# A block-sparse attention layer with two MLPs on one core: float64 weight words converted by whole blocks in place, their flush test from ScalarE's square, the first pass's low weight parts on VectorE

## The chip, the cores and the metric

The kernel runs on one core of a Trainium2 chip. The metric is the device time of one execution in microseconds (us); three runs gave 776.76 (median), 774.83 and 783.42.

## The reference

Three layers follow each other. First comes attention over 2 batches, 8 heads, 768 tokens and a head size of 64, in which a query sees only the keys that fall to the same of 16 centroids. Then comes a Fourier mixing with an MLP of width 2048, and last an MLP of width 1024 with a convolution of three taps and a gate:

```python
x = attn_out.transpose(0, 2, 1, 3).reshape(B, S, H * D)        # (2, 768, 512)
u = x + np.real(np.fft.fft(np.fft.fft(x, axis=1), axis=2))
un = (u - mean(u)) / np.sqrt(var(u) + 1e-06)
x = u + np.maximum(un @ w_ch1, 0.0) @ w_ch2                    # 512 -> 2048 -> 512
h = np.maximum(x @ w_in, 0.0)                                  # 512 -> 1024
conv_out = conv of h along the tokens, three taps per channel
out = (h * sigmoid(conv_out)) @ w_out                          # (2, 768, 512)
```

The weights of both MLPs and the taps come to the kernel as float64 (the draw makes them so), and are passed as pairs of 32-bit words.

## The kernel before, in words

**Stages.** Attention of all 16 heads is issued in an order written out by hand: 96 steps of 128 rows, and dictionaries (pre, mid, aft, post, fill) that hang other work on a step. Batch 0's mixing and normalisation are hung on the last third of these steps. Behind attention the order is made by the framework's planner: the program order is the priority, and the planner places each instruction in its engine's queue by its own estimate of when operands and buffers come free. Each engine then works its queue strictly in order.

**The wide MLP** goes in two passes, one per batch (g = 0, 1), over 16 weight blocks f. A block holds 128 columns of w_ch1 and 128 rows of w_ch2, as one tile of 128x1024. Precision comes from three matmuls in place of one (`pass3`, lines 75 to 78): high x high, high x low, low x high, where the high part is a value rounded to float32r and the low part the rest. `split_w` (line 763) makes the two weight parts: ScalarE casts the block (line 765), GpSimd subtracts (line 767). `mlp1_up` does 24 matmuls of 384 columns, ScalarE's ReLU gives the high part (line 781), VectorE subtracts for the low part (line 782). `down` does 18 matmuls of 512 columns into six banks. So a block of a pass has 42 matmuls. In pass 0 batch 1's mixing and normalisation are spread between the blocks (`later`): 30 matmuls for three `y` (lines 141 and before), 18 for two `z`, 7 and 39 for `a384` and three `ab`, and 24 transposes (line 261). Its folds, low parts and additions lie on VectorE and GpSimd (lines 104 to 222), its high parts on ScalarE (lines 113, 143, 145, 173). In pass 1 the second layer's transposes (`gate_in`) lie between the blocks. The last layer (`mlp2_up`, 8 blocks per batch) splits its blocks the same way.

**Conversion.** `from64` (line 273) makes float32 from the two words w0 (low) and w1 (high) of each float64. Its five VectorE steps are: the exponent and mantissa bits of w1, shifted, into a scratch tile `cvt` (line 277); the sign joined to it (278); the top three bits of w0 joined, into the target (279); w1 without its sign, into the scratch tile (281); a test of that against 0x38100000, multiplied with the target, so that what float32 could hold only as a denormal becomes zero (282). Lines 277 and 281 read one tensor, the others two. `load_w` (line 290) loads and converts a block in two halves of 512 columns, with three buffers `raw64` of 4 KB per partition and one scratch tile. Blocks a2 to a15 (the trace's `rawa`, `wa`) are converted in pass 0, blocks b0 to b7 of the last layer (`rawb`, `wb`) in pass 1. `NA` gives 2, 7 and 7 places for converted blocks; a9 to a15 use memory that batch 1's mixing gives up, and b0 and b1 take the places of a0 and a1 behind their last split. Blocks a0 and a1 are converted half by half during attention (`ahead_start`, line 660 on), a step of `from64` at each of five steps of the order, and go out to DRAM and back; a0's parts are made by `first_split`.

```python
AHEAD_STEPS = [12 * q + n for q in range(4) for n in (9, 10, 15, 17, 18)]
```

Of the kernel before, what the change touches and what calls it, by code (L numbers as in the profile page):

```python
# [12 lines left out]
I32 = mybir.dt.int32  # L13
U32 = mybir.dt.uint32
I64 = mybir.dt.int64
AF = mybir.ActivationFunctionType
ALU = mybir.AluOpType
# [8 lines left out]
AHEAD_STEPS = [12 * q + n for q in range(4) for n in (9, 10, 15, 17, 18)]  # L26
# [4 lines left out]
NT = S // 128  # L31
NH = B * H
BIG = float(2.0 ** 100)
P_SHIFT = 11

C_CS, C_SS, C_CD, C_SD, C_END = 0, 1158, 2310, 2826, 3342
# [4 lines left out]
def tile_net(ctx, tc, qk, v, cen, w12, w34, conv, dft, odd, out):  # L41
    nc = tc.nc
    V, A, G, T = nc.vector, nc.scalar, nc.gpsimd, nc.tensor

    def f32(ap):
        return ap.bitcast(F32)
# [13 lines left out]
    cbias = cp.tile([128, 1], F32, name="cbias")  # L60
    V.memset(cbias, float(P_SHIFT * np.log(2.0)))

    def pool(ctx_, name, bufs=1, side="left"):
        return ctx_.enter_context(tc.tile_pool(name=name, bufs=bufs, side=side, reuse_waits="tile"))
# [205 lines left out]
    NA = (2, 7, 7)  # L270
    wst, cvs, w32 = [], [], {}

    def from64(dst, raw, t):

        w0, w1 = (raw.rearrange("p (n t) -> p n t", t=2)[:, :, i] for i in range(2))
        return (
            lambda: V.tensor_scalar(t, w1, 3, 0x3FFFFFFF, ALU.logical_shift_left, ALU.bitwise_and),
            lambda: V.scalar_tensor_tensor(t, w1, -0x40000000, t, ALU.bitwise_and, ALU.bitwise_or),  # L278
            lambda: V.scalar_tensor_tensor(dst.bitcast(U32), w0.bitcast(U32), 29, t.bitcast(U32),  # L279
                                           ALU.logical_shift_right, ALU.bitwise_or),  # L280
            lambda: V.tensor_scalar(t, w1, 0x7FFFFFFF, None, ALU.bitwise_and),  # L281
            lambda: V.scalar_tensor_tensor(dst, t, float(0x38100000), dst, ALU.is_ge, ALU.mult),
        )

    def place_w(k, f):
        part = 0 if f < NA[0] else 1 if f < NA[0] + NA[1] else 2
        w32[k, f] = wst[part].tile([128, 1024], F32, tag="w32", bufs=NA[part], name=f"w{k}{f}")
        return w32[k, f]

    def load_w(k, f):  # L290
        w = place_w(k, f)
        for i in range(2):
            raw = cvs[0].tile([128, 1024], I32, tag="raw64", bufs=3, name=f"raw{k}{f}{i}")
            sl = slice(512 * i, 512 * i + 512)
            nc.sync.dma_start(out=raw.bitcast(I64), in_=(w12 if k == "a" else w34)[f][:, sl])
            for op in from64(w[:, sl], raw, cvs[0].tile([128, 512], I32, tag="cvt", bufs=1, name="cvt")):
                op()

    def up_half(o, w, x, i):
        tk = slice(384 * i, 384 * i + 384)  # L300
        for c in range(4):
            sl = slice(128 * c, 128 * c + 128)
            pass3(o, w[0][:, sl], w[1][:, sl], x[:, 0, c, tk], x[:, 1, c, tk], c == 0, c == 3)

    ws, hs, acc, xs, gps = {}, {}, {}, {}, []


    with ExitStack() as actx:
# [7 lines left out]
        def slot(name):  # L316
            turn[0] = (turn[0] + 1) % 3
            return ps.tile([128, 2, 512], F32, tag=f"s{turn[0]}", bufs=1, name=name)
# [37 lines left out]
        t = slot("warm_up")  # L356
# [22 lines left out]
        for i in range(2):  # L379
            t = ap.tile([128, NT, 2, 130], F16, name=f"V16_{i}")  # L380
# [30 lines left out]
        def prep_turn(m, t):  # L411
# [5 lines left out]
            A.copy(o[:, 0], po[0])  # L417
            A.activation(o[:, 1], po[1], AF.Copy, bias=-BIG, scale=BIG)
            d = ohD[m] = dr.tile([96, 2, 2, 128], F32, tag="ohd", name=f"ohd{m}")
            nc.sync.dma_start(out=d, in_=o)  # L420

        def first_mask():
# [6 lines left out]
            A.copy(Xs[0][64:80, 0], po[0])  # L429
            V.tensor_scalar(Xs[0][64:80, 1], po[1], BIG, -BIG, ALU.mult, ALU.add)  # L430

# [151 lines left out]
        def attn_out(hh, i):  # L583
            b, h = hh // 8, hh % 8
            r = avs[hh][:, 0:390].rearrange("p (t c) -> p t c", t=6)
            if i == 0:
                d = ds[hh] = ap.tile([128, 6], F32, tag="d", bufs=2, name=f"d{hh}")
                V.tensor_scalar(d, r[:, :, 64], float(2.0 ** P_SHIFT * 1e-9), None, ALU.add)
            elif i == 1:
# [9 lines left out]
        def at(where, step, *f):  # L599
            where.setdefault(step, []).append(f)  # L600

        for m in range(1, NH // 2):
            k = 12 * m - 24
# [45 lines left out]
        for i, t in enumerate((0, 3, 1, 4, 2, 5)):  # L649
            n = 72 + 3 * i  # L650
# [8 lines left out]
        def ahead_start(q):  # L659
            if q == 0:  # L660
                t = up_[0].tile([128, 8, S], F32R, tag="un", bufs=1, name="ahead")
                ahead["t"] = f32(t).rearrange("p a s -> p (a s)")
            t, f, i = ahead["t"], q // 2, q % 2
            raw = t[:, 1024 * i:1024 * i + 1024].bitcast(I32)
            nc.sync.dma_start(out=raw.bitcast(I64), in_=w12[f][:, 512 * i:512 * i + 512])
            dst = ahead[q] = t[:, 2560 + 512 * q:3072 + 512 * q]
            for n, op in zip(AHEAD_STEPS[5 * q:], from64(dst, raw, t[:, 2048:2560].bitcast(I32))):
                at(aft, n, op)

        def ahead_store(q):  # L670
# [7 lines left out]
        for q in range(AHEAD):  # L678
            at(pre, AHEAD_STEPS[5 * q] - 2, ahead_start, q)
            at(pre, AHEAD_STEPS[5 * q + 4] + 1, ahead_store, q)  # L680
# [45 lines left out]
        for n in range(-LEAD, 6 * NH + 10):  # L726
# [13 lines left out]
            if n in DFT_LOADS:  # L740
                i = DFT_LOADS.index(n)
# [10 lines left out]
    wp = pool(ctx, "wp", side="right")  # L752
    wst.append(pool(ctx, "wstA", side="right"))
    hctx = ctx.enter_context(ExitStack())
    hp = pool(hctx, "hp", side="right")
# [4 lines left out]
    def up_bank(name):  # L760
        return bank("up", 2, name)

    def split_w(p, bufs, k, f, name):
        wh = p.tile([128, 1024], F32R, tag="wh", bufs=bufs, name=f"wh{name}")
        A.copy(wh, w32[k, f])  # L765
        wl = p.tile([128, 1024], F32R, tag="wl", bufs=bufs, name=f"wl{name}")
        G.tensor_sub(wl, w32[k, f], f32(wh))  # L767
        return wh[:, 0:512], wl[:, 0:512], wh[:, 512:1024], wl[:, 512:1024]

    def mlp1_up(g, f):  # L770
        if (g, f) == (0, 0):
            h = hs[0, g, f] = [dp.tile([128, 780], F32R, tag=t, bufs=1, name=f"first{t}")[:, 0:S] for t in ("e0", "e1")]
            w = ws[0, g, f]
        else:
            h = hs[0, g, f] = [hp.tile([128, S], F32R, tag=t, bufs=3, name=f"{t}{g}_{f}") for t in ("hH", "hL")]
            w = ws[0, g, f] = split_w(hp, 3, "a", f, f"a{g}_{f}")
        for i in range(2):
            o = up_bank(f"up{g}_{f}_{i}")[:, 0:384]
            up_half(o, w, uns[g], i)
            tk = slice(384 * i, 384 * i + 384)  # L780
            A.activation(h[0][:, tk], o, AF.Relu)  # L781
            V.scalar_tensor_tensor(h[1][:, tk], o, 0.0, f32(h[0][:, tk]), ALU.max, ALU.subtract)  # L782
# [21 lines left out]
    def down(s, g, f, side, when=(2,)):  # L804
        w, h = ws.pop((s, g, f)), hs.pop((s, g, f))
        last = (15, 7)[s]
        if f == 0:
            acc[s, g] = [bank(f"acc{t}", 1, f"acc{s}{g}{t}") for t in range(NT)]
        for t in range(NT):
            sl = slice(128 * t, 128 * t + 128)  # L810
            pass3(acc[s, g][t], h[0][:, sl], h[1][:, sl], w[2], w[3], f == 0, f == last)
            if t in when and side:
                next(side, None)
            if f == last:
                if s == 0:
                    V.tensor_add(U[:, 6 * g + t], U[:, 6 * g + t], acc[s, g][t])
                else:
                    y = gps[0].tile([128, 512], F32, tag="y", bufs=3, name=f"y{g}{t}")
                    if t % 2:
                        V.tensor_copy(y, acc[s, g][t])  # L820
                    else:
                        A.copy(y, acc[s, g][t])
                    nc.sync.dma_start(out=out[g, 128 * t:128 * t + 128], in_=y)
# [41 lines left out]
    cw = wp.tile([128, 24], F32, tag="cw", bufs=1, name="cw")  # L865
    craw = wp.tile([128, 48], I32, tag="craw", bufs=1, name="craw")
    nc.sync.dma_start(out=craw.bitcast(I64), in_=conv)
    side = later()
    mlp1_up(0, 0)
    load_w("a", 2)  # L870
    for g in range(B):
        for f in range(16):
            if (g, f) < (B - 1, 15):
                mlp1_up(*((g, f + 1) if f < 15 else (g + 1, 0)))
            if (g, f) == (B - 1, 15):
                next(side, None)
            down(0, g, f, side, (1, 4) if g == 0 else (2,))
            if g == 0 and f + 3 < 16:
                load_w("a", f + 3)
            if g == 1 and 1 <= f < 9:  # L880
                load_w("b", f - 1)
            if (g, f) == (0, 15):
                side = gate_in(0)
            if (g, f) == (1, 9):
                for op in from64(cw, craw, wp.tile([128, 24], I32, tag="ccvt", bufs=1, name="ccvt")):
                    op()
    hctx.close()
    gps.append(pool(ctx, "gp", side="right"))
# [79 lines left out]
```

## Time and profile before

| | |
|---|---|
| median of three runs | 776.76 us |
| the profiled execution, its own time | 775.36 us |
| its span, first to last instruction | 773.6 us |
| TensorE matmul / VectorE / ScalarE / GpSimd busy | 703.1 / 581.5 / 314.8 / 358.3 us |
| mean granted TensorE clock | 0.974 |

The profile names engines PE (TensorE), PEld (its weight loads), DVE (VectorE), ACT (ScalarE), POOL (GpSimd) and SP (the DMA queue). Attention ends at about 305 us of the span, pass 0 at about 484, pass 1 at about 621. L279 is line 279 of the kernel. Busy times say little by themselves over the whole span, since the stages have different limits; the sections below look at single stages.

### The profile page before, as it was taken

How to read it: one execution, taken by the hardware profiler on the slowest of the kernel's cores; microseconds unless marked ns; L12 is line 12 of the kernel's file. 1: busy time of each engine (PE TensorE's matmuls, PEld its weight loads, DVE VectorE, ACT ScalarE, POOL GpSimd, SP SyncE). 2: the span in 40 equal slices, each digit the busy share in tenths (PEclk: the TensorE clock that was granted, in tenths of full speed). 3: DMA queues.
4: the chain of work that ended last, by engine and by line, in shares of the span. 5: the costliest groups of instructions: out<-in, count | busy, mean ns of one | idle time of the engine just before them, and what ended most of it. 6: DMA issues, size and time to landing. Idle time of an engine off the chain costs nothing.

```text
span 773.6 us, 12743 instructions
## 1 busy us (share of the span) xinstructions
PE 703.1 (91%) x5082; PEld 623.9 (81%) x5082; DVE 581.5 (75%) x864; ACT 314.8 (41%) x458; POOL 358.3 (46%) x231
## 2 busy tenths in 40 slices
PE   6899898997898897987998999999999989999996
PEld 5688797887797786876997789888999978888984
DVE  8668789898868999989669996999211167777763
ACT  2476667585457683222222212222222323333231
POOL 6276677577357765432353223222232155444441
PEclk9999999999899998988999999999999999999999
DMA  7768675552533330223203332231000000001002
GB/s 203 174 186 240 149 183 145 130 154 69 135 69 89 78 136 6 108 81 111 81 28 109 108 112 89 101 123 68 1 1 1 1 0 1 1 1 74 8 1 82
DMA packets 23107, 66.49 MB, mean 86 GB/s; under 512 B 3220, under 2 KB 6280, under 8 KB 22792
## 3 DMA queue, kind: packets, MB, share of 16 engines
q1 hardware_dynamic: 22616, 61.93, 27.9%
q0 software_dynamic: 432, 3.75, 1.4%
q8 instruction: 40, 0.66, 0.4%
q14 instruction: 19, 0.16, 0.1%
HBM read 40.94 MB, written 5.77 MB: 60 GB/s over the span
## 4 chain that ended last, share of the span: by engine, by line
PE 43%; DVE 40%; issue 5%; DMA 4%; POOL 4%; ACT 3%; SPq 1%; POOLq 0%; DVEq 0%; ACTq 0%
PE acc L76 4%; PE acc L78 4%; PE acc L77 4%; DVE cvt L278 4%; PE av L580 4%; DVE m L523 3%; DVE wa L279 3%; PE up L76 3%; PE s L518 3%; PE up L77 3%; PE up L78 3%; PE t L552 3%; DVE cvt L281 2%; PE t L554 2%; PE s L520 2%
## 5 line engine op out<-in xcount | busy, mean ns | idle before, releaser
L568 POOL TENSOR_TENSOR p<-p,p 128x768 f16<-128x768 f32 x76 | 135.4, 1787 | 80.2 <-ACT p L563 50.0
L767 POOL TENSOR_TENSOR wla<-wa,wha 128x1024 fp32r<-128x1024 f32 x31 | 79.4, 2562 | 172.7 <-ACT wha L765 172.7
L556 ACT ACTIVATE p<-t,cbias 128x768 f32<-128x768 f32 x96 | 86.3, 899 | 62.8 <-PE t L554 54.6
L523 DVE TENSOR_REDUCE m<-s 128x1 f32<-128x768 f32 x96 | 90.1, 944 | 14.8 <-PE s L520 14.2
L76 PE MATMUL up<-un,wha 128*128 128x384 f32 x248 | 86.1, 347 | 6.3 <-DVE Zy L152 5.2
L78 PE MATMUL up<-un,wla 128*128 128x384 f32 x248 | 84.6, 341 | 3.7 <-POOL wla L767 3.7
L77 PE MATMUL up<-un,wha 128*128 128x384 f32 x248 | 84.3, 340 | 0.0
L782 DVE SCALAR_TENSOR_TENSOR hL<-up,hH 128x384 fp32r<-128x384 f32 x62 | 34.2, 552 | 65.1 <-ACT hH L781 65.1
L580 PEld LDWEIGHTS <-p 128*128 128x128 f16 x1728 | 61.2, 100 | 22.3 <-issue 15.5
L580 PE MATMUL av<-V,p 128*128 128x65 f16 x1728 | 73.2, 197 | 6.1 <-POOL p L568 4.4
L563 ACT CAST p<-p 128x768 f16<-128x768 f32 x91 | 75.6, 831 | 1.6
L76 PE MATMUL acc<-wha,hH 128*128 128x512 f32 x186 | 74.1, 398 | 0.0
L77 PE MATMUL acc<-wla,hH 128*128 128x512 f32 x186 | 72.8, 391 | 0.0
L78 PE MATMUL acc<-wha,hL 128*128 128x512 f32 x186 | 72.7, 391 | 0.0
L552 PE MATMUL t<-X 128*128 128x384 f32 x192 | 55.6, 371 | 18.5 <-DVE m L523 17.6
L781 ACT ACTIVATE hH<-up 128x384 fp32r<-128x384 f32 x62 | 30.1, 490 | 96.3 <-PE up L78 96.3
L518 PE MATMUL s<-X 128*128 128x384 f32 x192 | 57.7, 382 | 8.3 <-DVE m L523 2.7
L765 ACT CAST wha<-wa 128x1024 fp32r<-128x1024 f32 x31 | 32.6, 1051 | 78.5 <-PE acc L78 42.4
L799 POOL TENSOR_TENSOR cv<-cv,h 128x768 f32<-128x768 f32 x16 | 25.4, 1591 | 78.1 <-ACT cv L798 78.1
L801 DVE CAST gH<-cv 128x768 fp32r<-128x768 f32 x16 | 35.3, 2208 | 31.3 <-POOL cv L799 28.7
L76 PEld LDWEIGHTS up<-un,wha 128*128 128x128 f32 x248 | 47.1, 190 | 11.3 <-DVE Zy L152 5.5
L552 PEld LDWEIGHTS t<-X 128*128 128x128 f32 x192 | 32.4, 195 | 25.4 <-DVE m L523 18.6
(310 smaller groups left out, 1684.2 us busy)
## 6 DMA issues: line engine op xcount, KB each, us to landing
rawa<-w SPq DMA_DIRECT2D x28, 512.0 KB
rawb<-w SPq DMA_DIRECT2D x16, 512.0 KB
raw<-qk SPq DMA_DIRECT2D x7, 768.0 KB
X<-G SPq DMA_DIRECT2D x14, 384.0 KB
Y<-G SPq DMA_DIRECT2D x14, 384.0 KB
DC<-dft POOLq DMA_DIRECT2D x2, 1671.0 KB, 9.1
vraw<-v SPq DMA_DIRECT2D x8, 384.0 KB
out<-y SPq DMA_DIRECT2D x12, 256.0 KB
```

Of the source, the lines that this page charges most:

```text
L76: T.matmul(o, sH, mH, start=start, stop=False)
L77: T.matmul(o, sH, mL, start=False, stop=False)
L78: T.matmul(o, sL, mH, start=False, stop=stop)
L518: T.matmul(t[:, c, 0:384], X[:, 0, sl], X[:, 1, 384 * c:384 * c + 384], start=True, stop=False)
L523: V.tensor_reduce(m6s[h][:, i:i + 1], t[:, :, 0:384], AX.XY, ALU.max, negate=True)
L552: T.matmul(t[:, c, 0:384], X[:, 1, sl], X[:, 0, 384 * c:384 * c + 384], start=True, stop=False)
L556: A.activation(p.rearrange("p (c n) -> p c n", c=2), t[:, :, 0:384], AF.Exp, bias=cbias, scale=0.125)
L563: A.copy(p16[:, 0], p32s[n])
L568: eng.tensor_sub(p16[:, 1], p, p16[:, 0])
L580: T.matmul(o, p16[:, k, 128 * j:128 * j + 128], v16[:, i, h % 2, 65 * part:65 * part + 65], start=(i + j + k + part == 0), stop=(i == 5), ...
L767: G.tensor_sub(wl, w32[k, f], f32(wh))
L801: V.tensor_copy(g[0], t)
```

## The change

Four things change. `from64` has no scratch tile: its first two steps write the target itself. Its fourth step, the mask on VectorE, goes; instead ScalarE squares w1, read as a float32, in place, ahead of the third step, and the last step tests the square against `LEAST` (the square of the float that has the bits 0x38100000, made smaller by 2^-16 of itself). `load_w` loads and converts a whole block of 1024 columns at a time, with two buffers of 8 KB per partition. `split_w` gets an engine for the subtraction: VectorE in pass 0, GpSimd in pass 1 and in the last layer. In attention the five steps of a half fall on the same five places: first, second, square, third, last.

```diff
+LEAST = float((1.125 * 2.0 ** -15) ** 2 * (1 - 2.0 ** -16))
...
-    def from64(dst, raw, t):
+    def from64(dst, raw):
...
+        d = dst.bitcast(I32)
         return (
-            lambda: V.tensor_scalar(t, w1, 3, 0x3FFFFFFF, ALU.logical_shift_left, ALU.bitwise_and),
-            lambda: V.scalar_tensor_tensor(t, w1, -0x40000000, t, ALU.bitwise_and, ALU.bitwise_or),
-            lambda: V.scalar_tensor_tensor(dst.bitcast(U32), w0.bitcast(U32), 29, t.bitcast(U32),
+            lambda: V.tensor_scalar(d, w1, 3, 0x3FFFFFFF, ALU.logical_shift_left, ALU.bitwise_and),
+            lambda: V.scalar_tensor_tensor(d, w1, -0x40000000, d, ALU.bitwise_and, ALU.bitwise_or),
+            lambda: A.activation(f32(w1), f32(w1), AF.Square),
+            lambda: V.scalar_tensor_tensor(dst.bitcast(U32), w0.bitcast(U32), 29, dst.bitcast(U32),
                                            ALU.logical_shift_right, ALU.bitwise_or),
-            lambda: V.tensor_scalar(t, w1, 0x7FFFFFFF, None, ALU.bitwise_and),
-            lambda: V.scalar_tensor_tensor(dst, t, float(0x38100000), dst, ALU.is_ge, ALU.mult),
+            lambda: V.scalar_tensor_tensor(dst, f32(w1), LEAST, dst, ALU.is_ge, ALU.mult),
         )
...
     def load_w(k, f):
         w = place_w(k, f)
-        for i in range(2):
-            raw = cvs[0].tile([128, 1024], I32, tag="raw64", bufs=3, name=f"raw{k}{f}{i}")
-            sl = slice(512 * i, 512 * i + 512)
-            nc.sync.dma_start(out=raw.bitcast(I64), in_=(w12 if k == "a" else w34)[f][:, sl])
-            for op in from64(w[:, sl], raw, cvs[0].tile([128, 512], I32, tag="cvt", bufs=1, name="cvt")):
-                op()
+        raw = cvs[0].tile([128, 2048], I32, tag="raw64", bufs=2, name=f"raw{k}{f}")
+        nc.sync.dma_start(out=raw.bitcast(I64), in_=(w12 if k == "a" else w34)[f])
+        for op in from64(w, raw):
+            op()
...
-    def split_w(p, bufs, k, f, name):
+    def split_w(p, bufs, k, f, name, eng=G):
...
-        G.tensor_sub(wl, w32[k, f], f32(wh))
+        eng.tensor_sub(wl, w32[k, f], f32(wh))
...
-            w = ws[0, g, f] = split_w(hp, 3, "a", f, f"a{g}_{f}")
+            w = ws[0, g, f] = split_w(hp, 3, "a", f, f"a{g}_{f}", (V, G)[g])
```

The other two calls of `from64` (in `ahead_start` and for the taps) lose their scratch tile in the same way.

## Rows read from the trace of the kernel before

**Rows 1.** Busy time by stretch: length, PE, PEld, DVE, ACT, POOL (instructions), PE clock, DMA

```profile
305.00:485.00 180.00, 164.20 (x835) 147.31 (x836) 154.46 (x246) 42.26 (x70) 64.19 (x36) 0.95 0.25 91
325.00:365.00 40.00, 29.92 (x130) 26.16 (x129) 36.89 (x52) 7.15 (x12) 14.45 (x7) 0.83 0.25 90
365.00:405.00 40.00, 40.00 (x223) 37.22 (x223) 26.17 (x53) 10.25 (x19) 17.36 (x13) 1.00 0.16 59
405.00:465.00 60.00, 54.36 (x275) 46.88 (x275) 58.56 (x90) 15.10 (x24) 17.19 (x8) 1.00 0.31 110
485.00:545.00 60.00, 57.06 (x291) 49.71 (x290) 57.48 (x88) 16.77 (x27) 17.21 (x7) 1.00 0.25 88
550.00:575.00 25.00, 25.00 (x128) 22.82 (x127) 3.34 (x6) 6.10 (x9) 7.19 (x3) 1.00 0.00 1
```

**Rows 2.** Chain of waits, 349 to 362 us: start, length, engine, output, line

```profile
352.06 2.73 DVE wa L279
...
356.45 0.56 DVE Zy L152
...
357.06 0.69 PE up L76
```

**Rows 3.** Waits, 305 to 485 us: who waited for whom, us in total, times, longest

```profile
ACT hH L781 <- PE up L78: 51.3, 23, 8.7
ACT wha L765 <- DVE wa L282: 33.9, 10, 7.5
PE up L76 <- DVE Zy L152: 5.2, 1, 5.2
PEld up L78 <- POOL wla L767: 5.0, 4, 2.1
DVE wb L279 <- POOL wla L767: 5.0, 1, 5.0
PEld y L76 <- ACT EH L113: 3.7, 1, 3.7
PEld y L78 <- POOL EL L117: 2.0, 1, 2.0
```

**Rows 4.** Busy time of conversion steps (tile `cvt`): first weights, then second

```profile
285.00:463.80 178.80, 106.46 (x140) 0.94 0.23 83
463.80:545.00 81.20, 58.30 (x81) 1.00 0.26 91
```

**Rows 5.** Tiles `rawa`, `wa`: ns minimum/median/maximum, first and last start, shape

```profile
L277 DVE TENSOR_SCALAR cvt<-rawa x28: 399/427/430, 288.8 to 460.4; 128x512 int32<-128x512 int32 x28
L279 DVE SCALAR_TENSOR_TENSOR wa<-rawa,cvt x28: 666/693/2837, 306.7 to 461.9; 128x512 uint32<-128x512 uint32 x28
L765 ACT CAST wha<-wa x31: 1036/1050/1058, 301.2 to 600.3; 128x1024 fp32r<-128x1024 f32 x31
L767 POOL TENSOR_TENSOR wla<-wa,wha x31: 2354/2466/3086, 304.2 to 601.5; 128x1024 fp32r<-128x1024 f32 x31
L692 DVE CAST firstYsH<-wa x1: 412/412/412, 300.8 to 300.8; 128x512 fp32r<-128x512 f32 x1
```

**Rows 6.** Instructions in order of time, 406 to 412 us: start, length, engine, line

```profile
407.69 2.35 POOL L767 TENSOR_TENSOR wla<-wa,wha 128x1024 fp32r<-128x1024 f32 x1 [4.91 <-ACT wha L765]
407.75 2.84 DVE L279 SCALAR_TENSOR_TENSOR wa<-rawa,cvt 128x512 uint32<-128x512 uint32 x1
```

**Rows 7.** Tile `G`: VectorE steps of 768 elements, columns as in rows 5

```profile
L443 DVE CAST G<-raw x7: 541/1610/2009, 5.5 to 236.8; 128x768 fp32r<-128x768 f32 x7
L448 DVE TENSOR_TENSOR G<-raw,G x7: 945/957/1055, 6.1 to 240.9; 128x768 fp32r<-128x768 f32 x7
```

**Rows 8.** Tile `rawa`, 310 to 315 us: length, DVE busy, PE clock, DMA share, GB/s

```profile
310.00:315.00 5.00, 3.40 (x6) 1.00 0.47 172
```

**Rows 9.** VectorE's groups by shape: count, busy us, mean ns

```profile
L281 DVE TENSOR_SCALAR ahead<-ahead 128x512 int32<-128x512 int32 x4 | 4.1, 1026 | 0.0
```

**Rows 10.** ScalarE's groups by shape

```profile
L798 ACT ACT_TABLE_LOAD x1 | 1.3, 1283 | 0.0
```

More of the change, by code (lines that the diff above doesn't have):

```diff
@@ L666, in ahead_start @@
             dst = ahead[q] = t[:, 2560 + 512 * q:3072 + 512 * q]
-            for n, op in zip(AHEAD_STEPS[5 * q:], from64(dst, raw, t[:, 2048:2560].bitcast(I32))):
+            for n, op in zip(AHEAD_STEPS[5 * q:], from64(dst, raw)):
                 at(aft, n, op)
@@ L884, in tile_net @@
             if (g, f) == (1, 9):
-                for op in from64(cw, craw, wp.tile([128, 24], I32, tag="ccvt", bufs=1, name="ccvt")):
+                for op in from64(cw, craw):
                     op()
```

## The prediction

> **What bounds the kernel now.** I read the time by stages first. In the first pass of the wide MLP (305 to 485 us) VectorE works 154.5 of 180 us and TensorE stands idle 15.8; TensorE's granted clock is 0.95 of the higher of its two levels (1.2 and 2.4 GHz) there, and 0.83 from 325 to 365, where 10.1 of the 15.8 idle us lie. From 405 to 465 VectorE works 58.6 of 60 us, TensorE 54.4. From 550 to 575, where VectorE has almost nothing to do, TensorE has no gap: 128 matmuls in 25 us, 0.195 us each, 8.2 us for the 42 of one weight block [rows 1].
>
> Next I ask what TensorE waits for. In the piece of the chain of waits from 349 to 362 us, conversion steps stand ahead of VectorE's small step on line 152, and TensorE resumes right behind it [rows 2]. The list of waits for the pass says the same: 5.2 us for line 152; ScalarE waits 33.9 us in 10 places for the last conversion step (line 282) before it can split the next block [rows 3]. So the pass is bound by VectorE's queue, not by TensorE's arithmetic. That arithmetic is 16 blocks x 8.2 = 131 us, 94 matmuls of batch 1's mixing and 24 transposes at no more than 0.195 = 23 [rows 1], in all 154. The pass has 26 us of slack: 15.8 of idle, 5 to 8 of low clock, the rest in gaps too short for the view.
>
> Then what fills VectorE: five conversion steps for each half block, 106.5 us for the first weights and 58.3 for the second [rows 4]. One half costs 0.43 + 3 x 0.69 + 0.43 = 2.93 us at the medians (the steps that read one tensor, lines 277 and 281, have one median, those that read two, lines 278, 279 and 282, the other), so 28 halves should take 82 us. The other 24.5 are steps that took up to 2.84 us [rows 5]. One of these shows why: GpSimd starts a weight subtraction at 407.69 and ends at 410.04; VectorE's line 279 starts at 407.75 and takes 2.84 instead of 0.69 [rows 6].
>
> **The change part by part.** *Whole blocks, one step fewer.* A step of 1024 has no row here. The one-source step goes from 0.41 (512, line 692) to 0.54 (768, line 443), 0.50 ns an element, so 0.43 + 512 x 0.50 = 0.69 us. The two-source steps go from 0.69 (512) to 0.96 (768), 1.04 ns an element, so 1.23 us [rows 5, 7]. A block then costs VectorE 0.69 + 3 x 1.23 = 4.4 us, where two halves cost 5.8. For 14 blocks this is 61; doubling the half steps gives 70, and no price per instruction would give 52. I take 61, since both slopes come from the nearest sizes. Against 106.5 this saves 45 us, of which 5 come back where GpSimd's mixing steps still stretch VectorE's.
>
> *Low weight parts on VectorE in the first pass.* Fifteen subtractions of 1024 at 1.23 add 18.5 us to VectorE and take 15 x 2.47 = 37 us off GpSimd [rows 5], and with them most of the stretching counted above. VectorE's busy time goes from 154.5 to 154.5 - 106.5 + 61 + 5 + 18.5 = 133 us (bounds 124 and 148) against TensorE's 154: it would no longer be the bound, but it would still be 87% full. The new subtraction waits for ScalarE's cast; behind it in VectorE's queue stand conversions and line 782, for which TensorE's next matmuls wait.
>
> *The square on ScalarE.* One square per block: 1.05 us by the cast of 1024 [rows 5], 14 x 1.05 = 15 us on an engine that is busy 42 of 180 us in the pass [rows 1]. It overwrites the words that VectorE's first two steps read, so it waits for them, and behind it stand ScalarE's ReLUs and casts; VectorE's last step waits for it, with line 782 behind. A wait of this kind has no row. Bounds: nothing, where the square runs beside the third step (1.05 under 1.23), and 8.7 us, the longest wait of a ReLU for TensorE [rows 3] with a square behind it. I take nothing, because ReLUs wait 2.2 us in the mean (51.3 over 23) and other VectorE steps can stand between.
>
> The Trainium skill's "ScalarE: Activation LUTs" (Rules for kernel authors) advises VectorE over ScalarE for simple arithmetic. Here the step leaves VectorE at 2 x 0.43 and costs ScalarE 1.05 [rows 5]: dearer, but on the idler engine. By that rule keeping it would cost VectorE 14 x 0.69 = 10 us in the pass and leave 143 of 154.
>
> *In place.* The first two steps now write the block's own place. For the first second-layer block that place was free only after GpSimd's subtraction; the third step waited 5.0 us for it, with VectorE idle [rows 3]. Now the first step waits there, with line 782 behind it; this idle time covers the two steps that can no longer go ahead, and I count nothing (without it, 0.69 + 1.23 = 1.9 us, once).
>
> *Transfers.* 22 issues of 1 MB replace 44 of half that, two buffers of 8 KB replace three of 4. The same bytes move. From 310 to 315 us the transfers ran at 172 GB/s with half of the engines' time unused [rows 8]; at that rate a block takes 6.1 us and two buffers give one each (4.4 + 6.1) / 2 = 5.3 us, under the 8.2 in which TensorE uses one. Cost nothing; at worst some 3 us ahead of the first block, covered by the two blocks that attention prepared.
>
> *Attention.* Line 281 (mean 1.03 us, four times) goes [rows 9], line 279 runs two steps later, and ScalarE gets four squares of 512. By the cast of 1024 one takes between 0.5 and 1.05 us [rows 5], so 2 to 4.2 us. ScalarE's queue feeds the exponentials, so the bounds are 4.2 lost and 4.1 won; I take 1 won, as these steps are on the end's path only some of the time.
>
> *Sum.* What does TensorE get back? From 325 to 365 it loses 10.1 idle and 5 of clock. The waits there begin with VectorE's queue, but ScalarE's cast (TensorE's weight load waited 3.7) and GpSimd's low part (2.0) stay in the mixing's chain [rows 3], so I take 9 of 15. From 405 to 465 it loses 5.6; I take 4.6. Of the other 5 us of slack I take 2. That is 15.6 in the first pass. In the second (485 to 545) VectorE is full as well, TensorE idle 2.9; conversions fall from 58 to 8 x 4.4 + 12 of stretching = 47, and I take 1.5. With attention's 1: 18 us. The profiled execution took 775.4 us, 1.4 under the median of the runs, so the sum is 775.4 - 18 = **757 us**.
>
> **The rivals.** *All slack returns.* If VectorE never leads again, the whole 26 come back, with 2.9 and 2: 744.5. For: 365 to 405 shows TensorE without a gap once conversions paused [rows 1]. Against: the mixing's chain through three engines remains.
>
> *The square's wait decides* (slower). Place: VectorE's last conversion step, behind a square that stands behind a ReLU waiting for TensorE. With w us per block the queue holds 133 + 14w; at w = 1.5 it is as full as before, at w = 3.4 it takes the present 180 us, and beyond that the pass is longer. At w = 4 it takes 189: 9 more, less 1 elsewhere, 783. For: ReLUs wait up to 8.7. Against: the mean of 2.2.
>
> *The low part comes late.* Today TensorE's weight loads wait 5.0 us in 4 places for GpSimd's subtraction [rows 3]; on VectorE it queues behind steps of 1.23. Below 1.24 us of queue it is early, since it is shorter by that much. With 2.2 of queue it is 1 us later in 15 blocks, and if TensorE stands still for each, 14 of the 18 go: 771. Against: three buffers let splits run ahead.
>
> *The mixing's own chain is the bound*: only 405 to 465 gains, 4.6 + 1.5 + 1: 768. Against: rows 2.
>
> *Table loads.* A load takes 1.28 us [rows 10]. If the square needed another table than the exponential, each of the four squares in attention would bring two loads, 10 us on a queue that is on the path: 767. The Trainium skill's "ScalarE: Activation LUTs" (Table sets: the hidden batching unit) says cheap functions sit in every set, yet does not name square among its examples; no row here shows a square.
>
> **How the numbers follow.** Forecast 0.60; all slack 0.13; the square's wait 0.07; late low part 0.10; mixing chain 0.07; table loads 0.03. One per cent, about what a measurement of this kernel can tell, is 7.8 us, so faster means under 769. Faster: the first two, the chain and the loads, less some of their spread: 0.80. Same: the late low part and that spread, 0.13. Slower: 0.07. The range is 745 to 770: it holds the forecast with its bounds (VectorE at 124 or 148 us moves it by about 8) and the nearer halves of its neighbours.
>
> **What would show it.** Right: the four conversion steps near 0.69 and 1.23 us, some 45 to 50 us less of them in the first pass; GpSimd without weight subtractions there; the pass about 164 us long; TensorE's idle near 6; the clock over 0.95 from 325 to 365. Wrong: long waits of VectorE's last step for the square, of TensorE for the new subtraction, more table loads than before, or a first pass still near 180 us with VectorE under 140 busy, which would mean that not its queue but the order of the mixing held TensorE.

## The result, and the profile after

The changed kernel takes 753.34 us in the median of four runs (751.96 to 753.71), the kernel before 779.36 in the median of four; the ratio is 0.966, with a 95% interval of 0.960 to 0.973. The forecast was 757 (745 to 770), faster. The profiled execution took 753.26 us, with a span of 751.5; before it was 775.36 and 773.6. So 22.1 of the 26.0 us between the medians lie between the two profiles: the profiled execution of the kernel before is 4.0 us under its median.

To see where the 22 us of span went I cut both traces at the same three events: TensorE's first matmul of the wide MLP, VectorE's first addition of the MLP's result to batch 0, and the same for batch 1. The first two rows are the two passes of the kernel before; the columns are start and end, length, then PE, PEld, DVE, ACT and POOL busy (instructions), PE clock, DMA share, GB/s.

```profile
305.58:483.56 177.98, 162.26 (x817) 145.51 (x814) 153.00 (x243) 41.78 (x69) 63.61 (x36) 0.95 0.25 90
483.56:617.58 134.02, 131.08 (x662) 117.01 (x661) 68.53 (x108) 36.73 (x55) 34.52 (x14) 1.00 0.12 42
```

The changed kernel, the same two passes and the stretch from 325 to 365 us:

```profile
304.68:465.36 160.68, 156.65 (x816) 142.66 (x814) 126.86 (x166) 59.66 (x85) 29.14 (x21) 0.99 0.27 99
465.36:594.43 129.07, 129.07 (x662) 117.78 (x661) 49.94 (x69) 43.23 (x61) 33.69 (x14) 1.00 0.12 42
325.00:365.00 40.00, 36.58 (x188) 32.82 (x187) 35.46 (x38) 13.96 (x20) 7.57 (x4) 1.00 0.36 132
```

The first pass is 17.3 us shorter, the second 4.9; attention ends 0.9 earlier, the last layer is 1.1 longer. In the first pass TensorE's idle time falls from 15.7 to 4.0, its own busy time from 162.3 to 156.7 with the clock at 0.99 for 0.95, and VectorE's busy time from 153.0 to 126.9. From 325 to 365 the clock is 1.00 where it was 0.83, and TensorE stands idle 3.4 us instead of 10.1 [rows 1]. GpSimd's busy time in the pass is 29.1 instead of 63.6.

The conversion steps of the first weights and the new subtraction, groups of VectorE by shape (count, busy us, mean ns, idle before):

```profile
L769 DVE TENSOR_TENSOR wla<-wa,wha 128x1024 fp32r<-128x1024 f32 x15 | 20.3, 1355 | 7.8 <-ACT wha L767 7.8
L284 DVE SCALAR_TENSOR_TENSOR wa<-rawa,wa 128x1024 uint32<-128x1024 uint32 x14 | 18.7, 1334 | 0.1
L282 DVE SCALAR_TENSOR_TENSOR wa<-rawa,wa 128x1024 int32<-128x1024 int32 x14 | 18.6, 1333 | 0.1
...
L286 DVE SCALAR_TENSOR_TENSOR wa<-rawa,wa 128x1024 f32<-128x1024 f32 x14 | 17.0, 1214 | 0.1
...
L281 DVE TENSOR_SCALAR wa<-rawa 128x1024 int32<-128x1024 int32 x14 | 10.9, 786 | 0.0
```

These four conversion steps take 65.2 us, where the five took 106.5 [rows 4]. Line 286 waits for the square, yet has 0.1 us of idle time in front of it. The waits of the pass (303 to 466 us; who waited for whom, us in total, times, longest):

```profile
ACT rawa L283 <- DVE wa L282: 13.7, 7, 6.1
...
ACT wha L767 <- DVE wa L286: 5.8, 4, 2.8
...
PEld up L80 <- DVE wla L769: 2.5, 3, 1.5
...
PEld y L80 <- POOL EL L119: 1.9, 1, 1.9
```

The reader should see two things: the square (line 283) waits for VectorE, never the other way; and ScalarE's wait for converted weights fell from 33.9 us to 5.8 [rows 3]. Part of what is left of TensorE's idle time shows the old trouble once more, in order of time:

```profile
325.68 2.60 POOL L119 TENSOR_TENSOR EL<-ev,EH 128x771 fp32r<-128x771 f32 x1 [3.96 <-ACT EH L115]
...
326.50 2.85 DVE L284 SCALAR_TENSOR_TENSOR wa<-rawa,wa 128x1024 uint32<-128x1024 uint32 x1
...
328.39 2.67 POOL L111 TENSOR_TENSOR ov<-U 128x765 f32<-128x765 f32 x1
...
329.28 2.87 DVE L769 TENSOR_TENSOR wla<-wa,wha 128x1024 fp32r<-128x1024 f32 x1
...
332.20 0.45 PE L80 MATMUL up<-un,wla 128*128 128x384 f32 x1 [1.14 <-DVE wla L769]
```

Two steps of GpSimd's mixing run, two of VectorE's steps of 1.22 us take 2.85 and 2.87 beside them, and TensorE waits 1.14 us for the second.

### The profile page after: what moved, and what is told of

The parts are those of the page before. It is cut to its first block, busy times and chain, and to the rows that moved or that the text cites. A ratio compares the mean times of both kernels' runs of the same rounds, so it can differ in the third digit from the quotient of the medians.

```text
span 751.5 us, 12570 instructions
## 1 busy us (share of the span) xinstructions
PE 700.7 (93%) x5082; PEld 628.9 (84%) x5082; DVE 531.3 (71%) x742; ACT 341.5 (45%) x485; POOL 320.9 (43%) x216
## 3 DMA queue, kind: packets, MB, share of 16 engines
q1 hardware_dynamic: 19448, 61.93, 28.6%
## 4 chain that ended last, share of the span: by engine, by line
PE 50%; DVE 33%; POOL 4%; issue 4%; DMA 4%; ACT 3%; SPq 1%; POOLq 0%; DVEq 0%; ACTq 0%
PE up L80 5%; PE up L78 5%; PE up L79 5%; PE acc L80 5%; PE acc L78 5%; PE acc L79 5%; DVE gH L803 5%; PE av L582 4%; DVE m L525 4%; POOL cv L801 3%; PE s L520 3%; PE t L554 3%; PE sim L393 3%; PE t L556 2%; PE s L522 2%
## 5 line engine op out<-in xcount | busy, mean ns | idle before, releaser
L769 POOL TENSOR_TENSOR wla<-wa,wha 128x1024 fp32r<-128x1024 f32 x16 | 38.5, 2406 | 126.5 <-ACT wha L767 126.5
L78 PE MATMUL up<-un,wha 128*128 128x384 f32 x248 | 84.1, 339 | 0.7 <-DVE YsL L178 0.5
L79 PE MATMUL up<-un,wha 128*128 128x384 f32 x248 | 83.8, 338 | 0.0
L582 PEld LDWEIGHTS <-p 128*128 128x128 f16 x1728 | 62.5, 101 | 22.8 <-issue 15.6
L582 PE MATMUL av<-V,p 128*128 128x65 f16 x1728 | 74.9, 199 | 6.3 <-POOL p L570 4.7
L554 PEld LDWEIGHTS t<-X 128*128 128x128 f32 x192 | 33.4, 199 | 24.3 <-DVE m L525 18.4
L556 PE MATMUL t<-Y 98*128 98x384 f32 x192 | 51.5, 350 | 1.1 <-DMA Y<-mr 1.0
```

What stands on the lines that cost most here:

```text
L78: T.matmul(o, sH, mH, start=start, stop=False)
L79: T.matmul(o, sH, mL, start=False, stop=False)
L554: T.matmul(t[:, c, 0:384], X[:, 1, sl], X[:, 0, 384 * c:384 * c + 384], start=True, stop=False)
L556: T.matmul(t[:, c, 0:384], Y[0:98, 1, sl], Y[0:98, 0, 384 * c:384 * c + 384], start=False, stop=True)
L582: T.matmul(o, p16[:, k, 128 * j:128 * j + 128], v16[:, i, h % 2, 65 * part:65 * part + 65], start=(i + j + k + part == 0), stop=(i == 5), ...
```

## The experiments

Each run is read by the same cuts. All times are medians of four runs (ten for attention_only) beside the kernel before on the same chip, 778 to 779.5; the passes are those of the profiled execution. In the 14 profiles the first matmul of the MLP starts anywhere from 301.5 to 310.6 us, with little or no difference in attention, so a part's effect of a few us is read from the passes, not from the totals. Each pass was profiled once. Two pairs of kernels share the code of both passes and agree there within 0.2 us: before and attention_only, changed and last_layer_on_vector.

| kernel | time | ratio to before | first pass: length, VectorE busy | second pass |
|---|---|---|---|---|
| before | 779.4 | | 178.0, 153.0 | 134.0 |
| changed | 753.3 | 0.966 (0.960 to 0.973) | 160.7, 126.9 | 129.1 |
| low_on_gpsimd | 765.4 | 0.985 (0.980 to 0.990) | 170.9, 125.0 | 129.0 |
| low_on_vector | 763.5 | 0.979 (0.972 to 0.985) | 161.8, 148.4 | 134.1 |
| mask_on_vector | 757.4 | 0.973 (0.970 to 0.976) | 160.7, 135.3 | 131.1 |
| halves | 756.7 | 0.972 (0.968 to 0.976) | 160.1, 129.8 | 130.4 |
| dummy_on_gpsimd | 771.2 | 0.989 (0.984 to 0.995) | 176.5, 150.1 | 130.4 |
| memset_on_gpsimd | 759.6 | 0.976 (0.972 to 0.979) | 163.2, 133.4 | 130.4 |
| sign_twice | 760.5 | 0.976 (0.971 to 0.981) | 163.8, 143.4 | 132.9 |
| no_flush | 755.7 | 0.970 (0.965 to 0.974) | 162.1, 108.5 | 129.1 |
| square_after_copy | 757.0 | 0.973 (0.969 to 0.977) | 161.3, 126.5 | 130.6 |
| attention_only | 777.0 | 0.998 (0.995 to 1.002) | 177.8, 152.9 | 134.0 |
| last_layer_on_vector | 748.7 | 0.962 (0.958 to 0.965) | 160.5, 126.7 | 129.1 |
| mixing_low_on_vector | 745.3 | 0.958 (0.954 to 0.961) | 159.1, 126.5 | 129.0 |

**The two halves of the change.** In the changed kernel:

```diff
-            w = ws[0, g, f] = split_w(hp, 3, "a", f, f"a{g}_{f}", (V, G)[g])
+            w = ws[0, g, f] = split_w(hp, 3, "a", f, f"a{g}_{f}", G)
```

> The changed kernel with the low weight parts of the first pass back on GpSimd. Theory A (the first pass follows the length of VectorE's own work; the conversion's 45 us less are the gain): VectorE loses 18.5 us of subtractions and gets some 20 of stretching back, stays under 140 us in the pass, and the time stays within 4 us of the changed kernel, 753 to 757. Theory B (the gain is the end of the stretching by GpSimd's subtraction): most of the gain goes, 768 to 775. Theory C (the planner's new order is what gained): no number, but the pass changes without VectorE's busy time changing.

It gave 765.4, between the theories. The first pass of this kernel:

```profile
306.48:477.40 170.92, 159.23 (x816) 143.78 (x814) 124.96 (x152) 59.48 (x85) 65.83 (x36) 0.98 0.27 93
```

This row is the one that theory A can't survive. VectorE is less busy than in the changed kernel (125.0 for 126.9), and the pass is 10.2 us longer. Its own sum is not what the pass follows. The planner's order changes in this run too, so it can't rule out theory C by itself; dummy_on_gpsimd below keeps the order. The steps show what the sum hides: line 286 takes up to 3.1 us where it took 1.23 at most. The columns here are count, minimum, median and maximum in ns, first and last start; first low_on_gpsimd:

```profile
L286 DVE SCALAR_TENSOR_TENSOR wa<-rawa,wa x14: 1209/1226/3135, 313.5 to 444.7; 128x1024 f32<-128x1024 f32 x14
```

and the changed kernel:

```profile
L286 DVE SCALAR_TENSOR_TENSOR wa<-rawa,wa x14: 1207/1215/1226, 311.5 to 436.2; 128x1024 f32<-128x1024 f32 x14
```

The other half, in the kernel before:

```diff
-    def split_w(p, bufs, k, f, name):
+    def split_w(p, bufs, k, f, name, eng=G):
...
-        G.tensor_sub(wl, w32[k, f], f32(wh))
+        eng.tensor_sub(wl, w32[k, f], f32(wh))
...
-            w = ws[0, g, f] = split_w(hp, 3, "a", f, f"a{g}_{f}")
+            w = ws[0, g, f] = split_w(hp, 3, "a", f, f"a{g}_{f}", (V, G)[g])
```

> The kernel before with only the first pass's low weight parts moved to VectorE. Theory A: VectorE gets 18.5 us more and some 24 of stretching less, 149 of the pass, so nearly full as before: 3 to 6 us faster than before, 771 to 775. Theory B: most of the gain is here, 755 to 760. If the subtraction queues behind conversions for longer than it saves: slower than before, 780 or more.

It gave 763.5 (755.2 to 765.7), neither's number, but nearer B. Its first pass:

```profile
301.52:463.33 161.81, 156.88 (x817) 140.49 (x814) 148.40 (x258) 42.68 (x69) 25.59 (x21) 1.00 0.28 99
```

This profile is of the fastest of the four executions, 8.3 us under their median, with attention ending 4.1 us earlier than in the profile of the kernel before; the gain by the medians, 15.9 us, agrees with its passes. VectorE is 92% full, and the first pass is as short as the changed kernel's within 1.1 us. So the moved subtraction alone gives 16.2 of the first pass's 17.3 us, the conversion alone 7.1, and together they give hardly more than the first. The second pass is the other way about: 134.1 with the old conversion, 129.0 with the new, whoever makes the first pass's low parts.

**Why GpSimd's subtraction costs so much.** This needed a kernel in which GpSimd works and nobody waits for it, with memory for a spare tile of 4 KB per partition. `halves` frees that much, with three buffers of 4 KB for two of 8:

```diff
-        raw = cvs[0].tile([128, 2048], I32, tag="raw64", bufs=2, name=f"raw{k}{f}")
-        nc.sync.dma_start(out=raw.bitcast(I64), in_=(w12 if k == "a" else w34)[f])
-        for op in from64(w, raw):
-            op()
+        for i in range(2):
+            raw = cvs[0].tile([128, 1024], I32, tag="raw64", bufs=3, name=f"raw{k}{f}{i}")
+            sl = slice(512 * i, 512 * i + 512)
+            nc.sync.dma_start(out=raw.bitcast(I64), in_=(w12 if k == "a" else w34)[f][:, sl])
+            for op in from64(w[:, sl], raw):
+                op()
```

> The changed kernel with blocks loaded and converted in two halves, three buffers of half the size. By the steps' fixed part VectorE gets 14 x 4 x 0.15 = 8 to 9 us more in the pass. Theory A: 2 to 5 us slower than the changed kernel, 755 to 758. If the size of the transfers or buffers were what counts: more than 6 slower or any faster.

It gave 756.7, as expected in the total but not for its reason: VectorE works 3.0 us more in the first pass, not 8 to 9, and the pass is no longer than the changed kernel's (160.1); the second is 1.3 longer. On top of it:

```diff
         eng.tensor_sub(wl, w32[k, f], f32(wh))
+        if eng is V:
+            spare = p.tile([128, 1024], F32R, tag="spare", bufs=1, name=f"spare{name}")
+            G.tensor_sub(spare, w32[k, f], f32(wh))
```

> The kernel with halves of before (756.7), with 15 subtractions of the same size on GpSimd in the first pass into a tile that nobody reads; VectorE still makes the low parts. Theory S (GpSimd's two-operand steps stretch VectorE's, and in the stretches where VectorE is full, 325 to 360 and 395 to 445, TensorE pays for it): the sum of VectorE's excess comes back, 15 to 25 us, and the time goes to 762 to 768. Theory L (what cost was the subtraction's own length on GpSimd, 2.47 for 1.23 us, which TensorE waited for): nobody waits for these, so 755 to 758.

In the two traces TensorE, VectorE, ScalarE and the DMA queue have exactly the same order of instructions; only GpSimd's queue differs, by the 15 spare steps. The two first passes, `halves`:

```profile
309.34:469.41 160.07, 156.05 (x814) 141.90 (x812) 129.82 (x229) 61.40 (x101) 25.82 (x21) 0.99 0.29 99
```

and dummy_on_gpsimd:

```profile
308.15:484.65 176.50, 161.29 (x814) 144.24 (x812) 150.06 (x228) 60.88 (x101) 68.91 (x36) 0.97 0.27 90
```

The same VectorE steps in the same order take 20.2 us more, and the pass is 16.4 us longer: nearly all that the change had won there. Of these 16.4, TensorE stands idle 11.2, and its matmuls take 5.2 longer, at a clock of 0.97 for 0.99. 771.2 is above what theory S expected (762 to 768), so its mechanism held and its price was too low. Taken step by step from the two traces, the 46 VectorE steps of the pass that ran beside a spare subtraction took 21.2 us more than the same steps in `halves`, and the other 182 together 1.8 us less. The waits of the pass say who paid. In `halves` (309 to 470 us):

```profile
DVE wb L281 <- POOL wla L771: 9.4, 2, 6.6
...
DVE st L244 <- POOL U L216: 3.6, 3, 1.2
...
PEld up L80 <- DVE wla L771: 2.5, 1, 2.5
...
DVE y L258 <- POOL rs L253: 1.5, 1, 1.5
PEld y L80 <- POOL EL L119: 1.5, 1, 1.5
```

and in dummy_on_gpsimd (308 to 485 us):

```profile
DVE wb L281 <- POOL wla L771: 9.4, 2, 6.6
...
PEld up L80 <- DVE wla L771: 4.1, 4, 1.7
...
DVE st L244 <- POOL U L216: 3.6, 3, 1.2
...
PEld up L78 <- DVE hL L789: 2.8, 2, 1.6
...
PEld up L78 <- DVE YsL L178: 2.6, 1, 2.6
...
DVE y L258 <- POOL rs L253: 1.5, 1, 1.5
...
PEld y L80 <- POOL EL L119: 0.5, 1, 0.5
```

VectorE waits for GpSimd exactly as long in both, and TensorE's weight loads wait less for it. What grew is the weight loads' waits for VectorE's results, 13.9 us in all for 3.9. The stretching of VectorE's steps was the cost, and neither a wait for the low part from GpSimd nor one for GpSimd's other work. Two kinds of step in dummy_on_gpsimd, from the views of two tiles:

```profile
L281 DVE TENSOR_SCALAR wa<-rawa x28: 381/416/2628, 309.3 to 458.8; 128x512 int32<-128x512 int32 x28
```

```profile
L789 DVE SCALAR_TENSOR_TENSOR hL<-up,hH x62: 518/557/559, 322.0 to 610.8; 128x384 fp32r<-128x384 f32 x62
```

A one-source step of 0.42 us takes up to 2.63; line 789, which reads one operand from PSUM and one from SBUF, never takes more than 0.56 in 62 instances. The Trainium skill's "GPSIMD Engine Reference" (Key points) says that GpSimd shares its SBUF interfaces with VectorE and contends with VectorE's instructions in a two-port mode or with two SBUF inputs. The runs agree for the steps with two SBUF inputs and for line 789, which has one and isn't stretched. Whether line 281 runs in a two-port mode no run here shows. The size is in the rows: line 281 grew by up to 2.2 us, beside spare subtractions of 2.4 to 3.4.

Another test of the same question: the mixing's own GpSimd steps stand behind the spare ones in GpSimd's queue. So GpSimd was kept busy without reading:

```diff
+        if eng is V:
+            spare = p.tile([128, 1024], F32, tag="spare", bufs=1, name=f"spare{name}")
+            for _ in range(2):
+                G.memset(spare, 0.0)
```

> As dummy_on_gpsimd, but GpSimd fills the spare tile twice with zeros (it reads nothing) in place of each spare subtraction. The order of every other engine's queue is the one of halves. Theory S (two-operand reads of GpSimd stretch VectorE's steps): if filling doesn't stretch them, the conversion steps keep their lengths and the time stays at 755 to 759. Theory Q (GpSimd's queue is what cost: the mixing's folds and low parts stand behind the spare work): 765 to 771 with unstretched steps. If filling stretches them too, this run tells nothing between the two.

It gave 759.6, just over the first range. Its first pass:

```profile
308.93:472.15 163.22, 157.64 (x814) 142.90 (x812) 133.38 (x228) 61.63 (x101) 54.37 (x51) 0.98 0.29 97
```

GpSimd is 28.6 us busier than in `halves` (43.1 in the run before), VectorE's steps take 3.6 us more, and the pass is 3.1 longer. The 50 VectorE steps beside a fill took 5.1 us more than in `halves`, the others 2.1 less. This run is a weaker test than it was meant to be: the fills are shorter in sum than the spare subtractions (29.7 us for 43.7), and since they wait for nothing, all start between 308 and 348 us, where the subtractions are spread from 308 to 463. That GpSimd's queue was not the cost rests on the waits above more than on this run.

**Plain work on VectorE.** As a counterpart, the same amount of time on VectorE without GpSimd: the second conversion step is done twice in `load_w`.

```diff
+        for n, op in enumerate(from64(w, raw)):
             op()
+            if n == 1:
+                op()
```

> The changed kernel with the second conversion step of each block in load_w done twice (the second time it changes nothing): 14 x 1.22 = 17 us more on VectorE in the first pass, 10 in the second, and nothing more on GpSimd. Theory A as predicted (VectorE counts by its sum over the pass: 127 + 17 = 144 of 161): 0 to 2 us slower than the changed kernel, 753 to 756. Theory A2 (VectorE is full in two stretches of the pass whatever its sum, since conversions run ahead there): 6 to 9 us slower, 759 to 763.

760.5 was expected by A2, but by its total alone: the first pass is 3.1 us longer for 16.5 us more of VectorE, the second 3.8 for 8.1. So neither A nor A2 has the size right. Beside dummy_on_gpsimd the contrast stands: 16.5 us of planned work cost the pass 3.1, 20.2 us of stretching cost it 16.4. One reading fits: the planner prices the doubled step and moves others around it (in the traces some 220 of TensorE's 5082 matmuls stand elsewhere in its order than in the changed kernel), while dummy_on_gpsimd moved none of them, though VectorE's steps were stretched by 20.2 us. That this is the reason wasn't tried.

**What else of the change counts.** The mask back on VectorE, in place, with the square left out:

```diff
-            lambda: A.activation(f32(w1), f32(w1), AF.Square),
+            lambda: V.tensor_scalar(w1, w1, 0x7FFFFFFF, None, ALU.bitwise_and),
...
-            lambda: V.scalar_tensor_tensor(dst, f32(w1), LEAST, dst, ALU.is_ge, ALU.mult),
+            lambda: V.scalar_tensor_tensor(dst, w1, float(0x38100000), dst, ALU.is_ge, ALU.mult),
```

> The changed kernel with the mask of the high word back on VectorE (one step of 1024 in place in the raw words) instead of ScalarE's square, which is left out. Theory A: 14 steps of 0.69 us, 10 us more on VectorE in the pass, most of it in the stretches where VectorE is full (305 to 360 and 390 to 435): 3 to 6 us slower than the changed kernel, 756 to 759. If the square's waits cost what the step saves: no difference, 752 to 754.

757.4, as theory A expected, but not for its reason: the first pass is the same 160.7 us, with 8.4 us more on VectorE; 2.0 us are in the second pass, and the rest of the difference between the two profiles lies ahead of the MLP. The flush test left out altogether:

```diff
-        for op in from64(w, raw):
+        for n, op in enumerate(from64(w, raw)):
+            if n in (2, 4):
+                continue
             op()
```

> The changed kernel with the flush test left out in load_w (the square and the last step): 17 us less on VectorE and 16 less on ScalarE in the first pass. If VectorE's queue still costs TensorE something there: 2 to 4 us faster than the changed kernel, 749 to 751. If the pass is now at TensorE's own length: within 1.5 of it, 752 to 755.

755.7 is nearest the second case, and 0.7 above its range: with 18.4 us less on VectorE the first pass isn't shorter (162.1) and the second is the same 129.1. Two steps less in VectorE's conversion shortened neither pass. And ScalarE's load doubled:

```diff
+            if n == 2:
+                w1 = f32(raw.rearrange("p (n t) -> p n t", t=2)[:, :, 1])
+                A.activation(w1, w1, AF.Copy)
             op()
```

> The changed kernel with a second step of ScalarE ahead of each square in load_w (a copy of the words onto themselves), 14 x 1.16 = 16 us more on ScalarE in the first pass and 9 in the second. The forecast's step (the square is hidden): within 2 us of the changed kernel, 752 to 755. The rival of the square's wait: VectorE's last step waits up to 1.2 us longer for each block, and behind it line 784: 758 to 768.

757.0 lies between the two cases; the passes (161.3 and 130.6) are 0.7 and 1.5 us longer, and line 286 waited for the square 1.4 us in all, in two places. So the square is hidden in the changed kernel, and a second step ahead of it costs little. Attention alone, in the kernel before: `ahead_start` uses the new `from64`, the rest the old one.

> The kernel before with only the four halves that attention converts done the new way (in place, with ScalarE's square). Predicted share: 1 us faster than before (bounds 4 either way). Theory: a difference under 3 us, 775 to 781 beside a before of 778. If attention had gained more than I took it for: under 774.

777.0, ratio 0.998 with an interval across one: what attention gained can't be told from nothing, between 3.7 us won and 1.2 lost.

**Versions that follow from this.** If GpSimd's two-operand steps are dear beside a VectorE that is needed, the last layer should gain too. Its casts of the gated values took 2.21 us in the mean:

```profile
L803 DVE CAST gH<-cv 128x768 fp32r<-128x768 f32 x16 | 35.4, 2213 | 31.3 <-POOL cv L801 31.3
```

```diff
-        w = ws[1, b, f] = split_w(gp, 4, "b", f, f"b{b}_{f}")
+        w = ws[1, b, f] = split_w(gp, 4, "b", f, f"b{b}_{f}", V)
```

> The changed kernel with the last layer's low weight parts on VectorE too. By theory S its casts of the gated values (2.21 us in the mean, 0.54 where nothing stretches them) lose 16 x 1.67 = 27 us, and VectorE gets 16 x 1.22 = 20: as these casts lie on the chain of waits (5 per cent of the span), 3 to 8 us faster than the changed kernel, 745 to 750. If only sums count: within 2 us, 751 to 755.

748.7, as expected, and the same casts in this kernel:

```profile
L803 DVE CAST gH<-cv 128x768 fp32r<-128x768 f32 x16 | 9.0, 560 | 31.3 <-POOL cv L801 28.7 <-PE u L80 2.6
```

The 26.4 us that they lose outweigh the 19.3 that the subtraction adds; what follows the second pass takes 148.7 us instead of 157.1. The casts are the likelier source of this than an earlier low part, for which TensorE's weight loads had waited only 1.9 us in this layer; the two weren't tried apart. With batch 1's mixing relieved as well:

```diff
-        for name, f in mixing(1, up_bank, lambda name: (up_bank(name + "b"), up_bank(name + "a")), G).items():
+        for name, f in mixing(1, up_bank, lambda name: (up_bank(name + "b"), up_bank(name + "a")), V).items():
```

> The kernel last_layer_on_vector with batch 1's mixing taken off GpSimd where a parameter allows it (two low parts and three mirrored additions), so that less on GpSimd stretches VectorE between 320 and 400 us. TensorE stands idle 2.9 us there from 325 to 335. Theory S: 1 to 3 us faster than last_layer_on_vector. If VectorE's queue has no room there: the same or up to 3 slower.

It gave 745.3, 3.4 us faster and so a little more than expected; from 325 to 365 us TensorE's idle time is 1.9 us where it was 3.5 in last_layer_on_vector:

```profile
325.00:365.00 40.00, 38.08 (x196) 34.28 (x195) 35.82 (x43) 15.19 (x22) 2.78 (x2) 1.00 0.36 132
```

The first pass is 1.4 us shorter; the rest of the difference between the profiles lies ahead of the MLP, where the two kernels do the same. This is the fastest kernel of the study, 4.2% under the kernel before.

## Why the prediction was right or wrong, point by point

- *The first pass is bound by VectorE's queue, and the change shortens it.* Right: 17.3 us, where 15.6 were forecast; idle 4.0 for the 6 expected, the clock 1.00 from 325 to 365. The time came out near partly by luck: the 15.6 were shares of TensorE's idle time and low clock, so they held although the working gave the wrong part of the change most of the credit.
- *VectorE's sum decides (133 of TensorE's 154, "87% full").* This step failed. low_on_gpsimd, whose conversion is the new one, has a smaller sum than the changed kernel and a pass 10.2 us longer; low_on_vector has 148.4, and a pass 1.1 longer. The pass follows where VectorE's steps are stretched, much more than how many us it works in all.
- *The prices of the steps.* Right: 1.22 and 0.69 us at the medians for the 1.23 and 0.69 estimated, 65.2 us for the 61 + 5 forecast.
- *The moved subtraction counted mainly as 18.5 us more, with "most of the stretching" going.* The mechanism was named, but credited to the wrong part: the conversion's 45 us hold the 24.5 of stretched time, of which the working gave 5 back. In low_on_vector, which keeps the old conversion, its five steps take 85.1 us for 106.5, so 21.4 went with GpSimd's subtraction. Measured, the moved subtraction is 16.2 of the pass's 17.3 us by itself, and putting only the stretching back costs 16.4.
- *The square is hidden.* Right: VectorE never waited for it, and a second step ahead of it cost the passes 0.7 and 1.5 us. The rival built on that wait had the waiting the wrong way round: ScalarE waits for VectorE, 13.7 us in 7 places.
- *Table loads.* None came with the square: there are two, of 1.28 us, as before. The Trainium skill's "ScalarE: Activation LUTs" (Table sets: the hidden batching unit) doesn't name square among the functions that sit in every set; here it needed no load, neither beside the exponential nor beside ReLU.
- *VectorE over ScalarE for simple arithmetic* (the Trainium skill's "ScalarE: Activation LUTs", Rules for kernel authors). By that rule 10 us of mask were forecast for VectorE; mask_on_vector shows 8.4 more, and no longer first pass. Here the rule costs 2.0 us in the second pass.
- *The low part comes late.* It stayed small: TensorE's weight loads waited 2.5 us in three places.
- *The second pass.* The term was mis-sized: 1.5 forecast, 4.9 measured. I had read only TensorE's 2.9 us of idle time as loss, and took half of it. In the changed kernel the pass has no gap in the view, and its 662 matmuls count 129.1 us of busy time where they counted 131.1: the other 2.0 us had stood in gaps too short for the view. The conversion won it: low_on_gpsimd has the short second pass, low_on_vector the long one.
- *Attention.* 1 forecast, 0.9 between the two profiles, and nothing measurable by itself.

## What to carry to other kernels

Look for VectorE steps whose maximum is far over their median, and for the GpSimd instruction that ran beside them: that excess is not spare time, and it delays whatever is queued behind it. Before giving a two-operand step to GpSimd because VectorE is busy, price it with what it would add to VectorE's steps; here 15 subtractions that nobody waited for cost 16.4 us. And don't judge an in-order queue by its sum over a stage: two kernels with 125 and 127 us of work differed by 10 us.

## What the runs showed of the hardware that was not expected

- A GpSimd step with two operands in SBUF made one-source VectorE steps as long as two-source ones: 0.42 to 2.63 us for a conversion step, 0.56 to 2.76 for the casts of the last layer. A step with one operand in PSUM stayed at its length.
- Filling a tile on GpSimd, 30 times 0.99 us, left VectorE's steps 3.6 us longer in sum, where 15 subtractions of 2.92 left them 20.2 longer.
- The square of 1024 words, every second word of the raw pairs, took 1.16 us on ScalarE (1.15 to 1.19), where the cast of 1024 took 1.05. The square itself isn't the reason: in square_after_copy a plain copy of the same words took 1.15 too.
